# W2 by column halves around batch 1's loads, half output tiles of batch 0, W1 means, folding and denominators in a new order, and batch 1's sums on GpSimd

## The chip, the cores and the metric

The kernel runs on one core of a Trainium2 chip. The metric is device time in microseconds (us), best when low. TensorE does the matmuls ("PE"; its weight loads are "PEld"), VectorE is "DVE", ScalarE "ACT", GpSimd "POOL". The mean clock granted to TensorE is given where it matters. Times of single steps come from the profiled execution, whose span is some 1.8 us shorter than the timed figure.

## The reference, cut to what matters

```python
# B=8 batches, H=8 heads, S=576, D=64, M=32 memory slots; C = H*D = 512, F = 2048
a = softmax(phi, over s)                     # (B,H,S,M)
k_m, v_m = pool(a, k), pool(a, v)            # "pooling": einsum bhsm,bhsd->bhmd
attn = softmax(q @ k_m.T / 8, over m)
x = (attn @ v_m), heads side by side         # (B,S,C): "context products"
xn = (x - mean) / sqrt(var + 1e-6) * g
out = x + relu(xn @ w_ch1) @ w_ch2           # w_ch1: C x F, w_ch2: F x C
```

## The kernel before: the parts that matter here

The kernel doesn't form `xn @ w_ch1` from x. It multiplies each batch's pooled V by W1 once ("folding", `w1b`), adds a term for the mean of W1's columns ("W1 means", `m_sb`), and then multiplies the folded W1 by the normalised attention weights `Eh` (512 products of 288 columns over all batches, `mm1`). `mm2` is the second layer, one output tile of 128 rows at a time, 16 matmuls each. Inputs of a batch are loaded one or two batches ahead. Batches 0 and 1 share tiles: batch 0 is folded while W1 still arrives, and its four output tiles run while batch 1's inputs arrive.

PSUM is handed out as three buffers of two banks ("big") and two of one bank ("one"):

```python
def big(shape, dtype, name):
    return psum.tile(shape, dtype, name=name, tag="big", bufs=3)
def one(shape, dtype, name):
    return psum.tile(shape, dtype, name=name, tag="one", bufs=2)

def w2_load(n):                                  # a quarter of W2's rows, all columns
    nc.gpsimd.dma_start(out=w2b[:, 4*n:4*(n+1), :], in_=w2_v[:, 4*n:4*(n+1), :])
# ... order on the load queue: batch 0, W1 (five pieces), W2, batch 1's phi, K, V, Q

def a_sum(b, ps):                                # sums of the exponents
    if b < 2:
        kv_sum(b, ps)                            # nine matmuls against ones
    else:                                        # GpSimd has added, two matmuls
        ...

# batch 0's W1 stage (cut)
    a_den(0, finish=False); a_tr(0, k_part=False)
    w1_mean(0); m_copy(0); a_w1b(0, 0, 0); a_den2(0)
    ...
    w1_mean(2); m_copy(2); a_w1b(0, 1); mm1(0, 2, 5)
    w1_mean(3); m_copy(3); a_w1b(0, 2); mm1(0, 5, 8)
    ...
# batch 0's output tiles among batch 1's attention (cut)
    mm2(0, 0, 4, 16); mm2(0, 1, 4, 16); mm2(0, 2, 0, 8)
    a_kv(1)                                      # pooling, with the sums first
    mm2(0, 2, 8, 12); a_tr(1); a_qT(1, 0); a_w1b(1, 0)
    mm2(0, 2, 12, 16, finish=False); a_qT(1, 1); a_w1b(1, 1); a_sc(1)
    ...
```

`w1_mean`, `mm2` and the fillers (`warm`, matmuls that only keep TensorE busy) use the one-bank buffers, nearly all else the two-bank ones.

The softmax here doesn't subtract the row's maximum and nothing guards it: scores larger than these inputs give would overflow.

## Time and profile before

| | before |
|---|---|
| time, median | 250.63 us (250.14 to 250.96, three runs; 250.8 over six) |
| span of the profiled execution | 248.8 us |
| TensorE busy | 236.5 us, 95% |
| first context product of batch 0 | 33.08 us |
| first product (`mm1`) of batch 1 | 53.65 us |
| batch 1's product until the next output tile | 8.65 us |

A profile line of the timeline gives start, length, engine, source line, operation, output<-inputs, shapes, count, and in brackets how long the engine stood idle before it and what ended that. The chain of waits follows the last instruction back to what released each step. A row of windows gives length, then busy time of PE, PEld, DVE, ACT and POOL with counts, clock, DMA share and GB/s. The prediction shows most lines that matter of before. Three more are the chain's sum by engine, and from TensorE's timeline the two waits for batch 1's inputs that the change is to remove:

```profile
PE 77%; DMA 17%; issue 2%; ACT 2%; POOL 1%; DVE 0%; POOLq 0%
```

```profile
42.95 0.80 PE L210 MATMUL kv_ps<-kv_bf,e_sb 64*32 64x128 bf16 x72 [0.22 <-DMA kv_bf<-in_v_dram]
...
45.20 0.73 PE L310 MATMUL qT_ps<-ident,q_bf 128*128 128x128 bf16 x10 [0.30 <-DMA q_bf<-in_q_dram]
```

The 17% of DMA is the first 45 us, in which loads keep the queue full.

### The profile page before, as it was taken

What the parts mean: (1) busy time and instruction counts of PE and PEld (TensorE: products, weight loads), DVE (VectorE), ACT (ScalarE), POOL (GpSimd) and SP (SyncE); (2) the same over time, 40 slices, a digit from 0 to 9 for tenths busy, and PEclk for the clock granted to TensorE, in tenths of its full rate; (3) what the DMA queues carried; (4) which work ended last, traced back from release to release, by engine and by line L of the source; (5) the groups of instructions that cost most, each with busy time, mean ns of one, the idle gap of its engine ahead of it and who ended that gap; (6) DMA issues with size and microseconds to landing.
All of it is one profiled execution on the core that took longest, in us unless ns stands there. A gap on an engine that the chain in (4) does not pass through costs nothing.

```text
span 248.8 us, 5860 instructions
## 1 busy us (share of the span) xinstructions
PE 236.5 (95%) x2460; PEld 132.2 (53%) x2491; DVE 156.0 (63%) x304; ACT 130.0 (52%) x219; POOL 60.7 (24%) x100
## 2 busy tenths in 40 slices
PE   7979899999999999999999999999999999999994
PEld 2544554457544665467544674466544764476442
DVE  3247663685577656687569637685679538783641
ACT  3164572587554465837472656655580755465310
POOL 8643241022325402090206202170205001000000
PEclk9999999999999999999999999999999999999999
DMA  7999999998499799919965997429983301203133
GB/s 150 190 202 206 207 256 213 286 223 148 119 174 236 116 216 245 179 20 194 262 122 117 146 242 168 104 37 221 211 167 68 73 14 43 45 12 75 42 84 84
DMA packets 42451, 36.82 MB, mean 148 GB/s; under 512 B 17461, under 2 KB 37689, under 8 KB 42425
## 3 DMA queue, kind: packets, MB, share of 16 engines
q0 software_dynamic: 17776, 19.53, 46.9%
q1 hardware_dynamic: 24488, 16.79, 28.4%
q8 instruction: 19, 0.31, 0.5%
q10 hardware_dynamic: 160, 0.13, 0.2%
q14 instruction: 8, 0.06, 0.1%
HBM read 41.42 MB, written 9.44 MB: 204 GB/s over the span
## 4 chain that ended last, share of the span: by engine, by line
PE 77%; DMA 17%; issue 2%; ACT 2%; POOL 1%; DVE 0%; POOLq 0%
PE ch_ps L481 45%; PE h_ps L411 22%; DMA q_bf<-in_q_dram 8%; DMA w1r<-in_moe_w_ch_dram 6%; DMA kv_bf<-in_k_dram 3%; PE w1b_ps L390 3%; PE o_ps L442 2%; PE last_ps L493 1%; ACT x_sb L448 1%; PE sc_ps L328 1%; PE den_ps L359 1%; PE kv_ps L210 1%; POOL q_bf L92 1%; PE qT_ps L310 0%; ACT qT L313 0%
## 5 line engine op out<-in xcount | busy, mean ns | idle before, releaser
L481 PE MATMUL ch_ps<-w2b,rT 128*128 128x512 bf16 x531 | 123.0, 379 | 2.3 <-issue 1.6
L481 PEld LDWEIGHTS <-rT 128*128 128x128 bf16 x560 | 52.1, 98 | 63.5 <-issue 6.5
L411 PE MATMUL h_ps<-Eh,w1b 128*128 128x288 bf16 x512 | 66.4, 285 | 1.3 <-ACT rT L417 1.0
L417 ACT ACTIVATE rT<-h_ps 128x576 bf16<-128x576 f32 x88 | 52.2, 648 | 26.8 <-PE h_ps L411 26.8
L411 PEld LDWEIGHTS <-w1b 128*128 128x128 bf16 x512 | 49.5, 97 | 18.1 <-issue 2.4
L394 DVE SCALAR_TENSOR_TENSOR w1b<-m_sb,rsum,w1b_ps 128x512 bf16<-128x512 f32 (+1 forms) x66 | 44.2, 726 | 8.5 <-PE w1b_ps L390 6.1
L419 DVE TENSOR_SCALAR rT<-h_ps 128x576 bf16<-128x576 f32 x40 | 30.3, 758 | 25.2 <-PE h_ps L411 24.6
L505 DVE SCALAR_TENSOR_TENSOR x_sb<-ch_ps,rstd,x_sb 128x512 f32<-128x512 f32 x35 | 26.1, 745 | 9.5 <-PE ch_ps L481 6.4
L461 DVE BATCH_NORM_STATS2 bst<-x_sb 128x6 f32<-128x512 f32 x36 | 24.3, 676 | 6.4 <-ACT x_sb L448 6.4
L448 ACT ACTIVATE x_sb<-o_ps 128x1024 f32<-128x1024 f32 (+1 forms) x20 | 17.8, 939 | 16.1 <-PE o_ps L442 16.0
L287 POOL TENSOR_TENSOR vb<-v,vmask 128x256 bf16<-128x256 bf16 x12 | 7.8, 664 | 60.9 <-DVE rs L237 60.9
L194 POOL TENSOR_TENSOR es<-e_sb 128x512 f32<-128x512 bf16 x6 | 6.9, 1156 | 62.2 <-ACT e_sb L187 62.2
L467 ACT ACTIVATE rstd<-mv,eps_sb 128x2 f32<-128x2 f32 (+1 forms) x20 | 5.9, 297 | 30.8 <-DVE mv L462 30.6
L333 ACT ACTIVATE E_sb<-sc_ps,rs 128x640 bf16<-128x640 f32 x16 | 11.8, 790 | 12.8 <-PE sc_ps L328 12.8
L375 DVE SCALAR_TENSOR_TENSOR Eh<-E_sb,rs,rden 128x576 bf16<-128x576 bf16 x16 | 12.4, 814 | 8.8 <-ACT rden L374 8.8
L179 PE MATMUL w_ps<-fill 128*128 128x512 f32 (+1 forms) x16 | 10.5, 774 | 1.6 <-DVE fill L119 1.6
L227 DVE CAST k<-kv_ps 128x256 bf16<-128x256 f32 x7 | 3.0, 425 | 13.8 <-PE kv_ps L210 13.8
L390 PE MATMUL w1b_ps<-w1r,kvT 64*32 64x512 bf16 (+1 forms) x264 | 10.9, 374 | 0.1
L187 ACT ACTIVATE e_sb<-phi_st 128x1152 bf16<-128x1152 f32 x8 | 9.2, 1151 | 2.7 <-DMA phi_st<-in_phi_dram 2.7
L374 ACT ACTIVATE rden<-rden 128x576 f32<-128x576 f32 x16 | 10.0, 672 | 0.1
L92 POOL DMA_DIRECT2D q_bf<-in_q_dram x10 | 7.6, 757 | 4.6 <-DMA w2b<-in_moe_w_ch_dram 1.8
L210 PE MATMUL kv_ps<-kv_bf,e_sb 64*32 64x128 bf16 (+1 forms) x648 | 7.4, 215 | 0.7 <-DMA kv_bf<-in_v_dram 0.4
(76 smaller groups left out, 150.9 us busy)
## 6 DMA issues: line engine op xcount, KB each, us to landing
out_dram<-x_sb SPq DMA_DIRECT2D x70, 128.0 KB, 2.9
kv_bf<-in_k_dram POOLq DMA_DIRECT2D x7, 576.0 KB, 6.1
kv_bf<-in_v_dram POOLq DMA_DIRECT2D x7, 576.0 KB, 9.5
phi_st<-in_phi_dram SPq DMA_DIRECT2D x6, 576.0 KB, 4.9
q_bf<-in_q_dram POOLq DMA_DIRECT2D x6, 576.0 KB, 13.6
w2b<-in_moe_w_ch_dram POOLq DMA_DIRECT2D x4, 512.0 KB, 17.8
w1r<-in_moe_w_ch_dram POOLq DMA_DIRECT2D x3, 512.0 KB, 14.2
q_bf<-in_q_dram POOLq DMA_DIRECT2D x4, 288.0 KB, 12.6
```

The costliest lines, as they stand in the source:

```text
L179: nc.tensor.matmul(w_ps[:, 0:N], fill[:, 0:P], fill[:, 0:N], start=True, stop=True)
L333: nc.scalar.activation(out=E_[:, g].rearrange("p (a x) -> p a x", a=2), in_=sc[:, :, 0:HP], func=AF.Exp, scale=s["rs"][:, g:g + 1])
L375: nc.vector.scalar_tensor_tensor(out=Eh[:, g, :], in0=s["E"][:, g, 0:S], scalar=s["rs"][:, g:g + 1], in1=rd[:, g].rearrange("p a x -> p (a ...
L390: nc.tensor.matmul(ps[32 * j:32 * (j + 1), g, 0:N], s["kvT"][r:r + 64, 2, 32 * j:32 * (j + 1)], w1r[r:r + 64, j, fs], start=True, stop=Tru ...
L394: nc.vector.scalar_tensor_tensor(out=s["w1b"][:, g, fs], in0=m_sb[:, fs], scalar=s["rsum"][:, g:g + 1], in1=ps[:, g, 0:N], op0=ALU.mult, o ...
L411: nc.tensor.matmul(h_ps[:, half, 0:HS], s["w1b"][:, g, P * j:P * (j + 1)], s["Eh"][:, g, HS * half:HS * (half + 1)], start=(g == 0), stop= ...
L417: nc.scalar.activation(out=dst, in_=h_ps[:, :, 0:HS], func=AF.Relu)
L419: nc.vector.tensor_scalar(out=dst, in0=h_ps[:, :, 0:HS], scalar1=0.0, scalar2=None, op0=ALU.max)
L448: nc.scalar.activation(out=x[:, 0:n].rearrange("p i (u y) -> p i u y", u=2), in_=o_ps.rearrange("p u (i y) -> p i u y", i=2)[:, 0:n], func ...
L461: nc.vector.bn_stats(out=stt, in_=x)
L481: nc.tensor.matmul(ch_ps, rT[:, j, P * t:P * (t + 1)], w2b[:, j, :], start=(j == 0), stop=(j == JC - 1))
L505: nc.vector.scalar_tensor_tensor(out=x, in0=ch_ps, scalar=rstd, in1=x, op0=ALU.mult, op1=ALU.add)
```

## The change

The intent: batch 1's V and Q should not have to queue behind all of W2, of which batch 0's first output tiles need one half only. So W2 is loaded by column halves, the second half behind batch 1's Q, and batch 0's four tiles are computed as eight half tiles, all first halves ahead of batch 1's attention. At the same time batch 0's W1 stage is reordered (means and folding a piece ahead of the products, folding into the one-bank buffers), the denominators go head half by head half, and batch 1's sums of exponents move to GpSimd.

```diff
-    def w2_load(n):
-        nc.gpsimd.dma_start(out=w2b[:, 4 * n:4 * (n + 1), :], in_=w2_v[:, 4 * n:4 * (n + 1), :])
+    def w2_load(h, n):
+        nc.gpsimd.dma_start(out=w2b[:, 4 * n:4 * (n + 1), C2[h]],
+                            in_=w2_v[:, 4 * n:4 * (n + 1), C2[h]])
...
     for n in range(4):
-        w2_load(n)
+        w2_load(0, n)
     phi1 = load_phi(1, nc.gpsimd)
     kv1 = load_kv(1)
     q1 = load_q(1)
     loaded[1] = (phi1, kv1, q1)
+    for n in range(4):
+        w2_load(1, n)
...
-        if b >= 2:                    # GpSimd adds the exponents
+        if b >= 1:
...
-        if b < 2:
+        if b < 1:
             kv_sum(b, ps)
...
+        if ones:                      # folding into both one-bank buffers
+            ps = [one([P, 512], FP32, "w1b_ps") for _ in range(2)]
...
+    def mm2h(t, h, j0, j1):           # half an output tile
+        if j0 == 0 and (h == 1 or t % 2 == 0):
+            halfs[h] = one([P, 2, C // 2], FP32, "ch_ps")
...
-    w1_mean(2); m_copy(2); a_w1b(0, 1); mm1(0, 2, 5)
-    w1_mean(3); m_copy(3); a_w1b(0, 2); mm1(0, 5, 8)
+    mm1(0, 2, 4, (0,)); w1_mean(2); m_copy(2); mm1(0, 2, 4, (1,)); a_w1b(0, 1, ones=True)
+    w1_mean(3); m_copy(3); mm1(0, 4, 6); a_w1b(0, 2, ones=True)
...
+    mm2h(2, 0, 0, 16); mm2h(3, 0, 0, 16); mm2h_out(2, 0); mm2h_out(3, 0)
+    a_kv(1); a_qT(1, 0); a_tr(1); a_qT(1, 1)
+    mm2h(0, 1, 0, 4); a_sc(1); a_w1b(1, 0); load(2)
...
+    a_eh(1, 1); a_w1b(1, 2)
+    mm2h(0, 1, 12, 16); mm2h_out(0, 1)
+    mm2h(1, 1, 12, 16); mm2h_out(1, 1)
+    mm2h(2, 1, 0, 16); a_exp(2); a_w1b(1, 3)
+    mm2h(3, 1, 0, 16); mm2h_out(2, 1); a_vb(1); mm2h_out(3, 1)
```

(Statements that stand on lines of their own are joined here, comments are added, and lines are cut.)

More of the change, by code (lines that the diff above doesn't have):

```diff
@@ L102 @@
     w2_v = moe_w_ch2.rearrange("(j p) c -> p j c", p=P)
-    def w2_load(n):
-        nc.gpsimd.dma_start(out=w2b[:, 4 * n:4 * (n + 1), :], in_=w2_v[:, 4 * n:4 * (n + 1), :])
+    C2 = (slice(0, C // 2), slice(C // 2, C))
+    def w2_load(h, n):
+        nc.gpsimd.dma_start(out=w2b[:, 4 * n:4 * (n + 1), C2[h]],
+                            in_=w2_v[:, 4 * n:4 * (n + 1), C2[h]])
     phi0 = load_phi(0)
@@ L261, in a_tr @@
         s = st8[b]
-        t_ps = big([P, 3, P], BF16, "kvT_ps")
+        t_ps = (big if k_part else one)([P, 3, P], BF16, "kvT_ps")
         if k_part:
@@ L335, in a_sc, with den_tiles @@
         s["E"] = E_
-    def a_den(b, finish=True):
+    def den_tiles(b):
         s = st8[b]
-        Eh = att.tile([P, 2, S], BF16, name="Eh", bufs=3)
-        rd = att.tile([P, 2, 2, HS], FP32, name="rden", bufs=1)
-        if b < 2:
-            for g in range(2):
-                den = big([P, 2, 512], FP32, "den_ps")
-                for half in range(2):
-                    o = HS * half
-                    nc.tensor.matmul(den[:, half, 0:HS], blk, s["E"][:, g, o:o + HS],
-                                     start=True, stop=True)
-                nc.scalar.activation(out=rd[:, g], in_=den[:, :, 0:HS], func=AF.Ln)
-        else:
-            den = [big([P, 2, 512], FP32, "den_ps") for _ in range(2)]
-            E_ = s["E"]
-            for half in range(2):
-                cs = slice(HS * half, HS * (half + 1))
-                for r in (0, D):
-                    for g in range(2):
-                        o = r if g == 0 else D - r
-                        nc.tensor.matmul(den[g][o:o + D, half, 0:HS], blk[r:r + D, r:r + D],
-                                         E_[r:r + D, g, cs], start=True, stop=True,
-                                         tile_position=(r, o))
-            nc.scalar.activation(out=rd[:, 0], in_=den[0][:, :, 0:HS], func=AF.Ln)
-            for r in (0, D):
-                nc.scalar.activation(out=rd[r:r + D, 1], in_=den[1][D - r:P - r, :, 0:HS],
-                                     func=AF.Ln)
-        s["Eh"], s["rd"] = Eh, rd
-        if finish:
-            a_den2(b)
@@ new lines, in den_tiles, with a_den_g @@
+        s["Eh"] = att.tile([P, 2, S], BF16, name="Eh", bufs=3)
+        s["rd"] = att.tile([P, 2, 2, HS], FP32, name="rden", bufs=1)
+        return s["rd"]
+    def a_den_g(b, g):
+        s = st8[b]
+        rd = den_tiles(b) if g == 0 else s["rd"]
+        den = big([P, 2, 512], FP32, "den_ps")
+        for half in range(2):
+            o = HS * half
+            nc.tensor.matmul(den[:, half, 0:HS], blk, s["E"][:, g, o:o + HS],
+                             start=True, stop=True)
+        nc.scalar.activation(out=rd[:, g], in_=den[:, :, 0:HS], func=AF.Ln)
+        nc.scalar.activation(out=rd[:, g], in_=rd[:, g], func=AF.Exp, scale=-1.0)
@@ new lines, in a_den @@
+    def a_den(b):
+        rd = den_tiles(b)
+        den = [big([P, 2, 512], FP32, "den_ps") for _ in range(2)]
+        E_ = st8[b]["E"]
+        for half in range(2):
+            cs = slice(HS * half, HS * (half + 1))
+            for r in (0, D):
+                for g in range(2):
+                    o = r if g == 0 else D - r
+                    nc.tensor.matmul(den[g][o:o + D, half, 0:HS], blk[r:r + D, r:r + D],
+                                     E_[r:r + D, g, cs], start=True, stop=True,
+                                     tile_position=(r, o))
+        nc.scalar.activation(out=rd[:, 0], in_=den[0][:, :, 0:HS], func=AF.Ln)
+        for r in (0, D):
+            nc.scalar.activation(out=rd[r:r + D, 1], in_=den[1][D - r:P - r, :, 0:HS],
+                                 func=AF.Ln)
@@ L370, in a_den2, with a_eh @@
+    def a_eh(b, g):
+        s = st8[b]
+        nc.vector.scalar_tensor_tensor(
+            out=s["Eh"][:, g, :], in0=s["E"][:, g, 0:S],
+            scalar=s["rs"][:, g:g + 1], in1=s["rd"][:, g].rearrange("p a x -> p (a x)"),
+            op0=ALU.mult, op1=ALU.mult)
     def a_den2(b):
-        s = st8[b]
-        Eh, rd = s["Eh"], s["rd"]
+        rd = st8[b]["rd"]
         for g in range(2):
             nc.scalar.activation(out=rd[:, g], in_=rd[:, g], func=AF.Exp, scale=-1.0)
-            nc.vector.scalar_tensor_tensor(
-                out=Eh[:, g, :], in0=s["E"][:, g, 0:S],
-                scalar=s["rs"][:, g:g + 1], in1=rd[:, g].rearrange("p a x -> p (a x)"),
-                op0=ALU.mult, op1=ALU.mult)
@@ L380, in a_w1b @@
-    def a_w1b(b, n, part=None):
+            a_eh(b, g)
+    def a_w1b(b, n, part=None, ones=False, evict=True):
         s = st8[b]
@@ L383, in a_w1b @@
             s["w1b"] = att.tile([P, 2, F], BF16, name="w1b", bufs=1)
-        ps = big([P, 2, 512], FP32, "w1b_ps")
+        if ones:
+            ps = [one([P, 512], FP32, "w1b_ps") for _ in range(2)]
+        else:
+            ps2 = big([P, 2, 512], FP32, "w1b_ps")
+            ps = [ps2[:, g] for g in range(2)]
         fs = slice(512 * n, 512 * (n + 1)) if part is None else W1C[part]
@@ L390, in a_w1b, with out, mm1_g, mm1 @@
                 nc.tensor.matmul(
-                    ps[32 * j:32 * (j + 1), g, 0:N], s["kvT"][r:r + 64, 2, 32 * j:32 * (j + 1)],
+                    ps[g][32 * j:32 * (j + 1), 0:N], s["kvT"][r:r + 64, 2, 32 * j:32 * (j + 1)],
                     w1r[r:r + 64, j, fs], start=True, stop=True, tile_position=(r, 32 * j))
-        for g in range(2):
+        def out(g):
             nc.vector.scalar_tensor_tensor(
                 out=s["w1b"][:, g, fs], in0=m_sb[:, fs], scalar=s["rsum"][:, g:g + 1],
-                in1=ps[:, g, 0:N], op0=ALU.mult, op1=ALU.add)
+                in1=ps[g][:, 0:N], op0=ALU.mult, op1=ALU.add)
+        if not evict:
+            return out
+        for g in range(2):
+            out(g)
     pair = {}
-    def mm1(b, j0, j1):
+    hs = {}
+    def mm1_g(b, j, g):
         s = st8[b]
-        if b % 2 == 0 and j0 == 0:
+        if g == 0:
+            hs[j] = big([P, 2, 512], FP32, "h_ps")
+        for half in range(2):
+            nc.tensor.matmul(
+                hs[j][:, half, 0:HS], s["w1b"][:, g, P * j:P * (j + 1)],
+                s["Eh"][:, g, HS * half:HS * (half + 1)],
+                start=(g == 0), stop=(g == 1))
+    def mm1(b, j0, j1, gs=(0, 1)):
+        if b % 2 == 0 and j0 == 0 and 0 in gs:
             pair[b // 2] = moe.tile([P, JC, 2 * S], BF16, name="rT", bufs=1)
@@ L407, in mm1 @@
         for j in range(j0, j1):
-            h_ps = big([P, 2, 512], FP32, "h_ps")
-            for g in range(2):
-                for half in range(2):
-                    nc.tensor.matmul(
-                        h_ps[:, half, 0:HS], s["w1b"][:, g, P * j:P * (j + 1)],
-                        s["Eh"][:, g, HS * half:HS * (half + 1)],
-                        start=(g == 0), stop=(g == 1))
+            for g in gs:
+                mm1_g(b, j, g)
+            if 1 not in gs:
+                continue
+            h_ps = hs[j]
             dst = rT[:, j, off:off + S].rearrange("p (a x) -> p a x", a=2)
@@ L484, in mm2, with mm2h_out @@
             mm2_out(pr, t)
+    halfs = {}
+    def mm2h(t, h, j0, j1):
+        if j0 == 0 and (h == 1 or t % 2 == 0):
+            halfs[h] = one([P, 2, C // 2], FP32, "ch_ps")
+        if j0 == 0:
+            chs[(t, h)] = halfs[h][:, 0 if h else t % 2, :]
+        for j in range(j0, j1):
+            nc.tensor.matmul(chs[(t, h)], pair[0][:, j, P * t:P * (t + 1)],
+                             w2b[:, j, C2[h]], start=(j == 0), stop=(j == JC - 1))
+    def mm2h_out(t, h):
+        x, rstd = xs[(0, t)]
+        nc.vector.scalar_tensor_tensor(out=x[:, C2[h]], in0=chs[(t, h)],
+                                       scalar=rstd, in1=x[:, C2[h]], op0=ALU.mult, op1=ALU.add)
+        if h == 1:
+            x_out(0, t, x)
     def mm2_last(pr, t):
@@ L506, in mm2_out, with x_out @@
                                        op0=ALU.mult, op1=ALU.add)
+        x_out(pr, t, x)
+    def x_out(pr, t, x):
         for u in range(2):
@@ L534 @@
     v_out(0, v_ps[:, :, 0:D])
-    a_den(0, finish=False)
+    a_den_g(0, 0)
     a_tr(0, k_part=False)
+    a_den_g(0, 1)
     w1_mean(0)
     m_copy(0)
-    a_w1b(0, 0, 0)
-    a_den2(0)
-    warm(1, 256)
+    fold = a_w1b(0, 0, 0, evict=False)
+    fold(0)
+    a_eh(0, 0)
+    fold(1)
+    a_eh(0, 1)
+    warm(1)
     w1_mean(1)
     m_copy(1)
-    a_w1b(0, 0, 1)
-    warm(1, 256)
-    mm1(0, 0, 2)
+    mm1(0, 0, 2, (0,))
+    a_w1b(0, 0, 1, ones=True)
+    mm1(0, 0, 2, (1,))
+    mm1(0, 2, 4, (0,))
     w1_mean(2)
     m_copy(2)
-    a_w1b(0, 1)
-    mm1(0, 2, 5)
+    mm1(0, 2, 4, (1,))
+    a_w1b(0, 1, ones=True)
     w1_mean(3)
     m_copy(3)
-    a_w1b(0, 2)
-    mm1(0, 5, 8)
+    mm1(0, 4, 6)
+    a_w1b(0, 2, ones=True)
+    mm1(0, 6, 8)
     w1_mean(4)
     m_copy(4)
-    a_w1b(0, 3)
-    mm1(0, 8, 11)
+    mm1(0, 8, 9)
+    a_w1b(0, 3, ones=True)
     a_vb(0)
-    mm1(0, 11, 16)
+    mm1(0, 9, 16)
     x_tiles(0, [0, 1])
     x_tiles(0, [2, 3])
-    mm2(0, 0, 0, 4)
-    mm2(0, 1, 0, 4)
+    mm2h(0, 0, 0, 16)
     x_rstd(0, [0, 1])
+    a_exp(1)
+    mm2h(1, 0, 0, 16)
+    mm2h_out(0, 0)
+    mm2h_out(1, 0)
     x_rstd(0, [2, 3])
-    a_exp(1)
-    mm2(0, 0, 4, 16)
-    mm2(0, 1, 4, 16)
-    mm2(0, 2, 0, 8)
+    mm2h(2, 0, 0, 16)
+    mm2h(3, 0, 0, 16)
+    mm2h_out(2, 0)
+    mm2h_out(3, 0)
     a_kv(1)
-    mm2(0, 2, 8, 12)
+    a_qT(1, 0)
     a_tr(1)
-    a_qT(1, 0)
+    a_qT(1, 1)
+    mm2h(0, 1, 0, 4)
+    a_sc(1)
     a_w1b(1, 0)
-    mm2(0, 2, 12, 16, finish=False)
-    a_qT(1, 1)
+    load(2)
+    mm2h(1, 1, 0, 4)
+    mm2h(0, 1, 4, 8)
+    a_den_g(1, 0)
     a_w1b(1, 1)
-    a_sc(1)
-    mm2_out(0, 2)
-    mm2(0, 3, 0, 4)
-    a_w1b(1, 2)
-    a_den(1)
-    load(2)
+    mm2h(1, 1, 4, 8)
+    a_den_g(1, 1)
+    a_eh(1, 0)
+    mm2h(0, 1, 8, 12)
+    mm2h(1, 1, 8, 12)
+    a_eh(1, 1)
+    a_w1b(1, 2)
+    mm2h(0, 1, 12, 16)
+    mm2h_out(0, 1)
+    mm2h(1, 1, 12, 16)
+    mm2h_out(1, 1)
+    mm2h(2, 1, 0, 16)
     a_exp(2)
-    mm2(0, 3, 4, 12)
     a_w1b(1, 3)
-    mm2(0, 3, 12, 16, finish=False)
+    mm2h(3, 1, 0, 16)
+    mm2h_out(2, 1)
     a_vb(1)
-    mm2_out(0, 3)
+    mm2h_out(3, 1)
     a_qT(2, 0)
@@ L651 @@
         if more:
-            a_den(nb, finish=False)
+            a_den(nb)
         mm2_out(pr, t[1])
```

## The prediction

> **What bounds the kernel now.** I read the page first, then the chain of waits, then windows and timelines of the stretch that the change touches.
>
> ```profile
> PE 236.5 (95%) x2460; PEld 132.2 (53%) x2491; DVE 156.0 (63%) x304; ACT 130.0 (52%) x219; POOL 60.7 (24%) x100
> ```
>
> TensorE (PE) is busy nearly throughout, so only its idle time, or time given to useless work, can be won. The chain says where that lies:
>
> ```profile
> 10.52 15.11 DMA w1r<-in_moe_w_ch_dram
> 25.62 0.29 issue
> 25.91 19.24 DMA q_bf<-in_q_dram
> 45.15 0.05 issue
> 45.20 0.73 PE qT_ps L310 x10
> ...
> 53.81 0.57 PE h_ps L411 x4
> 54.39 0.02 issue
> 54.41 0.66 ACT rT L417
> 55.07 0.04 issue
> 55.11 7.13 PE h_ps L411 x56
> ```
>
> Columns: start, length, what held the chain. Up to 45 us it runs through the load queue (W1, W2, then batch 1's phi, K, V, Q, in order); after that it is PE. From the first product of batch 1 (h_ps, 53.65) on, PE is full, and the diff leaves that part alone. So the change is decided by when PE reaches this product, and by how well it then runs. Two windows split the start at the first context product of batch 0 (33.1):
>
> ```profile
> 16.40:33.10 16.70, 15.34 (x131) 8.88 (x132) 12.38 (x22) 9.96 (x18) 5.22 (x8) 1.00 1.25 206
> 33.10:53.65 20.55, 19.71 (x234) 9.77 (x237) 12.17 (x25) 11.55 (x19) 2.55 (x4) 1.00 1.18 248
> ```
>
> (PE, PEld, DVE, ACT, POOL busy, clock, DMA share, GB/s.) The clock is full. PE's busy time counts pipeline latency, so I count issue time. First window: W1 means 3.5 us (8 matmuls of 0.115, 12 of 0.216), folding 1.5, fillers 0.9, 64 products of 0.124 are 8.0: 13.9 of 16.7. Second: 64 output matmuls of 0.216 are 13.8, all else some 5.6: 19.4 of 20.55. So 2.8 and 1.1 us are the most that better order could give, 1.6% together.
>
> **What the Trainium skill says.** "TensorE: Matmul & The Clock Gate", Back-to-back issue gap: a warm matmul of N columns takes N/2.4 + 2.5 ns alone, and streams with weight loads have other figures (131 ns at N=512). The trace agrees with the first: 8 output matmuls take 1.73 us in the chain (216 ns at 512), 64 products 7.96 us (124 ns at 288). So I take 0.1105 us at 256: halving a tile costs only 0.005 us a pair. "PSUM — Partial Sum Buffer", Engine vs sequencer instructions: the queues of VectorE, ScalarE and GpSimd are strict FIFO. The timelines show these engines in program order; my prediction rests on it. The same page, Specifications (TRN2): 8 banks of 2 KiB. The code has 3 buffers of two banks and 2 of one: all 8 are taken, so whoever takes a one-bank buffer takes it from another. "DMA: Bandwidth & Descriptors", Specifications: at least 512 B for line rate. W2 halves write rows of 512 B, just there. The trace's packets of the first two W1 pieces, of that size, take 59 ns, those of 1024 B 95 ns: 196 against 206 GB/s in 2 us stretches. Halving W2 costs some 0.5 us of queue.
>
> **The change part by part.**
>
> *Loads.* W2's second halves go behind batch 1's Q. W1 is in at 25.6; four halves of about 1.3 us, phi 1.55 (as now), K 2.65, V and Q some 6: V lands near 38 (now 42.9), the Qs near 39 and 41 (now 45.15 and 47.1), W2 complete near 46. The DMA wait in the chain goes. That is the intent, and I believe it.
>
> *Batch 0's W1 stage.* The same matmuls, but now folding takes both one-bank buffers, which the W1 means use too. I followed the three engines by hand, folding 0.70 us (0.44 at 256 columns), evictions 0.65 on ACT and 0.76 on DVE, copy of means 0.60. Denominators by halves bring Eh's first half to 18.7 (now 19.2), its second stays at 19.95. Then: 0.45 waiting for that half; 0.35 for the first eviction (the fourth open h tile needs a fourth big buffer); 0.35 for the copy of means that frees the second fold buffer; 0.95 for the fold that frees the bank of the third means (PE done 23.4, fold until 24.3); 0.3 for the copy of the last means; 0.35 before piece 13; with 0.35 before the first Eh, 3.1 idle against 2.8 now. The last W1 piece lands at 25.6 and is not used before 27. The stage ends at 33.4, now 33.1: no gain.
>
> *Batch 0's first halves.* Context products 0.65, 64 matmuls of 0.1105 are 7.1: PE is at batch 1's pooling 7.7 us after the stage's end, at 41.1. But batch 1's sums of exponents now come from GpSimd instead of nine matmuls (saves 0.3), and the pooling waits for them first. Their way now, from ACT and POOL timelines:
>
> ```profile
> 36.58 0.29 ACT L467 ACTIVATE rstd<-mv,eps_sb 128x2 f32<-128x2 f32 x1 [0.86 <-DVE mv L462]
> ```
>
> ```profile
> 54.04 1.16 POOL L194 TENSOR_TENSOR es<-e_sb 128x512 f32<-128x512 bf16 x1 [15.65 <-ACT e_sb L187]
> 55.28 0.94 POOL L196 TENSOR_TENSOR es<-es 128x256 f32<-128x256 f32 x1
> 56.30 0.45 POOL L197 TENSOR_TENSOR es<-es 128x128 f32<-128x128 f32 x1
> 56.83 0.43 POOL L198 TENSOR_TENSOR es<-es,e_sb 128x128 f32<-128x128 f32 x1
> 57.32 0.29 POOL L200 CAST hl<-es 128x128 bf16<-128x128 f32 x1
> 57.70 0.43 POOL L201 TENSOR_TENSOR hl<-es,hl 128x128 bf16<-128x128 f32 x1
> ```
>
> The rstd starts 3.5 us after the stage's end (behind copies and statistics). The exponential follows it: 0.5 + 1.15. The six GpSimd steps (here batch 2's) run from 54.04 to 58.13, 4.1 us. Sum with hand-overs 9.4 us: PE waits 9.4 - 7.7 = 1.7 us. Pooling starts at 42.8 (now 42.2 for the sums, 42.95 for K and V): what the loads gave is taken by this.
>
> *Second halves.* From pooling (t = 0): pooling 0.8, key copy on ACT until 1.3, first Q transposes until 1.45, their copy of 1.24 until 2.8, the next 0.7 until 3.5. The scores need both, and PE has only transposes and four half matmuls before: 0.7 us idle. First folding at 3.85. Then PE goes through two folding pieces, two denominators, 24 half matmuls, a third folding and 8 more, until 8.5. DVE has two pairs of folds (1.4 each), Eh's halves (0.8 each, the second behind ACT's four passes, 8.0), then the third pair:
>
> ```profile
> 46.34 1.40 DVE L394 SCALAR_TENSOR_TENSOR w1b<-m_sb,rsum,w1b_ps 128x512 bf16<-128x512 f32 x2 [0.73 <-PE w1b_ps L390]
> ...
> 52.37 1.55 DVE L375 SCALAR_TENSOR_TENSOR Eh<-E_sb,rs,rden 128x576 bf16<-128x576 bf16 x2 [0.70 <-ACT rden L374]
> ```
>
> 4.35 to 7.25 for two pairs, Eh until 8.85, third pair until 10.25, and only then the output of tile 0's second half, about 0.43, until 10.7. Tile 2's second half needs its bank: the second halves are four one-bank tiles in two buffers. PE stands from 8.5 to 10.75, 2.25 us. Then 1.8 + 0.35 + 1.8: batch 1's product starts at 14.6.
>
> *Sum.* 33.4 + 9.4 + 14.6 = 57.4, now 53.65: 3.75 later. In return batch 1's product no longer stops after two tiles (8.65 us until the next outputs at 62.3, against 7.96 in batch 2), as exponentials, folds and Eh are done before it: 0.65 back. Cross-check: idle 1.7 + 0.7 + 2.25 against 1.1 now is +3.5, halves +0.25, sums -0.3, stage +0.3, the product -0.65: 3.1 us slower. 250.63 + 3.1 = 253.7; as the intent speaks the other way and my count of 17 us by hand can err by a microsecond, I say 253.3.
>
> **Rivals.** (1) The intent holds: the DMA wait goes and nothing takes its place. For it: the chain's 19 us on Q. Against it: PE had only some 0.3 us idle for Q, because W2 work filled the wait. It would need all waits removed: 248 to 250. (2) Only one of the two new waits is real, say because GpSimd finishes sooner or DVE gets to the output earlier: 251 to 252. Both follow from program order and measured durations, so this is less likely. (3) The W1 stage gets faster: idle down to half, 1.5 us less, hence 252. (4) It gets slower, with DVE late for evictions, or 256-column matmuls take 0.13 for their weight loads: 2.5 us for 128, 255.5 to 256. PE's 64-odd ns transposes with as many weights speak against that.
>
> **Range and chances.** The two waits give 4 us, the W1 stage is open to +-1. From one wait gone and a better stage to both in full with a worse stage: 250.8 to 255.4. 2% is 5.0 us. Faster by that needs more than all idle time there is (3.9): 0.02. Slower needs 1.5 us beyond my sum: 0.09. Within: 0.89.
>
> **What would show it.** PE's gap before batch 1's pooling with GpSimd's last sum as releaser (1.7); its gap before the third second-half tile with DVE as releaser (2.2); V and Q of batch 1 landing before PE is ready; 16 half matmuls in 1.77 us; the stage of batch 0 ending at 33.4; batch 1's product starting near 57.4 and taking 8.0; later stages shifted, alike. I am wrong if pooling starts at once after the first halves, if a DVE backlog doesn't hold tile 2, or if the first product starts before 53.

## The result, and the profile after

The changed kernel takes 254.0 us (median of six runs, 253.78 to 257.24); before took 250.8 us in the same rounds. The ratio is 1.0157, 95% interval 1.0116 to 1.0197. Ratios here are the mean time of one kernel's runs over that of the other's of the same rounds, so not quite the ratio of the medians. Four of the six runs lie between 253.78 and 254.08; the others, 255.64 and 257.24, had a mean clock of 0.99 and 0.987.

Page of the changed kernel, busy times and the chain by engine:

```profile
PE 237.0 (94%) x2519; PEld 138.3 (55%) x2546; DVE 156.8 (62%) x308; ACT 130.3 (52%) x219; POOL 66.9 (27%) x110
...
PE 81%; ACT 6%; DVE 4%; DMA 4%; POOL 3%; issue 2%; POOLq 0%; DVEq 0%
```

TensorE does 0.5 us more in a span 3.3 us longer. DMA has fallen from 17% of the chain to 4%: the loads are no longer what the chain runs through. In its place stand ACT, DVE and POOL. The chain of the changed kernel shows where (start, length, what):

```profile
37.82 1.06 ACT e_sb L192
...
38.96 1.16 POOL es L199
...
42.39 0.44 POOL hl L206
...
43.05 0.73 PE kv_ps L215 x72
...
50.94 0.82 DVE Eh L378
51.76 1.32 DVE w1b L408 x2
53.08 0.41 DVE x_sb L527
...
53.53 1.91 PE ch_ps L522 x16
...
57.63 7.96 PE h_ps L427 x64
```

First: exponential, GpSimd's additions, and only then batch 1's pooling. Second: `Eh`, a pair of folds and the output of tile 0's second half on DVE, and only then TensorE's tile 2. After 57.63 it is TensorE alone, as before. The timeline of TensorE in the changed kernel puts numbers to these waits and shows a third, in the W1 stage:

```profile
24.53 1.02 PE L170 MATMUL m_ps<-w1r,gneg 128*128 128x512 bf16 x4 [0.93 <-DVE w1b L408]
...
33.79 0.71 PE L470 MATMUL o_ps<-vb,Eh 64*128 64x128 bf16 x16
34.44 7.16 PE L522 MATMUL ch_ps<-w2b,rT 128*128 128x256 bf16 x64
42.36 0.18 PE L256 MATMUL kv_ps<-ones,hl 128*128 128x2 bf16 x1 [0.76 <-POOL hl L205]
42.87 0.18 PE L256 MATMUL kv_ps<-ones,hl 128*128 128x2 bf16 x1 [0.33 <-POOL hl L206]
...
53.53 1.91 PE L522 MATMUL ch_ps<-w2b,rT 128*128 128x256 bf16 x16 [1.88 <-DVE x_sb L527]
```

The bracket counts from the end of the last result in the pipeline; from the last matmul's issue the gaps are a little longer. The 64 first-half matmuls follow each other at 0.109 us and end their issue near 41.5, and pooling starts at 42.98: 1.5 us, less one tiny matmul between. The gap before tile 2 is some 2.0 us.

Adding up by the profiles' landmarks, changed minus before: the scores of batch 0, which nothing changed, start 0.17 later (14.36 against 14.19, loads differ that much from run to run); from there to the first context product 19.43 against 18.89, +0.54; from that to batch 1's first product (57.46 against 53.65) 23.67 against 20.57, +3.10; that product until the next output tile 8.18 against 8.65, -0.47 (both profiles lack the record of that tile's first matmul, 7 of 8 are there; in e1_kvsum, where it is there, the distance is 7.95, so the true ones are some 0.2 shorter and the difference stands); the remainder 186.46 against 186.50. The sum is +3.3, the difference of the spans (252.1 and 248.8).

### The profile page after: what moved, and what is told of

Its sections match the earlier page's. It is cut to its first block, busy times and chain, and to the rows that moved or that the text cites. A ratio compares the mean times of both kernels' runs of the same rounds, so it can differ in the third digit from the quotient of the medians.

```text
span 252.1 us, 5995 instructions
## 1 busy us (share of the span) xinstructions
PE 237.0 (94%) x2519; PEld 138.3 (55%) x2546; DVE 156.8 (62%) x308; ACT 130.3 (52%) x219; POOL 66.9 (27%) x110
## 4 chain that ended last, share of the span: by engine, by line
PE 81%; ACT 6%; DVE 4%; DMA 4%; POOL 3%; issue 2%; POOLq 0%; DVEq 0%
PE ch_ps L509 42%; PE h_ps L427 25%; DMA kv_bf<-in_v_dram 4%; PE w1b_ps L403 3%; PE ch_ps L522 2%; PE o_ps L470 2%; ACT x_sb L476 2%; PE last_ps L539 1%; PE kv_ps L215 1%; PE sc_ps L333 1%; PE m_ps L170 1%; ACT rT L445 1%; DVE w1b L408 1%; PE den_ps L368 1%; DVE Eh L378 1%
## 5 line engine op out<-in xcount | busy, mean ns | idle before, releaser
L509 PE MATMUL ch_ps<-w2b,rT 128*128 128x512 bf16 x470 | 108.5, 379 | 2.0 <-issue 1.4
L509 PEld LDWEIGHTS <-rT 128*128 128x128 bf16 x496 | 46.2, 98 | 56.4 <-issue 5.8
L551 DVE SCALAR_TENSOR_TENSOR x_sb<-ch_ps,rstd,x_sb 128x512 f32<-128x512 f32 x31 | 23.1, 745 | 7.5 <-PE ch_ps L509 4.5
L199 POOL TENSOR_TENSOR es<-e_sb 128x512 f32<-128x512 bf16 x7 | 8.1, 1155 | 57.8 <-ACT e_sb L192 57.8
L522 PE MATMUL ch_ps<-w2b,rT 128*128 128x256 bf16 x128 | 15.3, 273 | 1.9 <-DVE x_sb L527 1.9
L522 PEld LDWEIGHTS <-rT 128*128 128x128 bf16 x128 | 12.1, 98 | 4.5 <-issue 3.1
L232 DVE CAST k<-kv_ps 128x256 bf16<-128x256 f32 x7 | 3.0, 425 | 13.8 <-PE kv_ps L215 13.8
L403 PE MATMUL w1b_ps<-w1r,kvT 64*32 64x512 bf16 (+1 forms) x264 | 11.5, 374 | 0.0
L184 PE MATMUL w_ps<-fill 128*128 128x512 f32 x14 | 9.9, 828 | 1.6 <-DVE fill L122 1.6
```

Of the source, the lines that this page charges most:

```text
L403: nc.tensor.matmul(ps[g][32 * j:32 * (j + 1), 0:N], s["kvT"][r:r + 64, 2, 32 * j:32 * (j + 1)], w1r[r:r + 64, j, fs], start=True, stop=Tru ...
L509: nc.tensor.matmul(ch_ps, rT[:, j, P * t:P * (t + 1)], w2b[:, j, :], start=(j == 0), stop=(j == JC - 1))
L522: nc.tensor.matmul(chs[(t, h)], pair[0][:, j, P * t:P * (t + 1)], w2b[:, j, C2[h]], start=(j == 0), stop=(j == JC - 1))
L551: nc.vector.scalar_tensor_tensor(out=x, in0=ch_ps, scalar=rstd, in1=x, op0=ALU.mult, op1=ALU.add)
```

## The experiments

Theory: the time comes from two new waits, one for GpSimd's sums (A), one for a bank behind DVE's work (B), and a little from the W1 stage (C); the new order of loads itself works. Rivals: the waits are only symptoms and would come back elsewhere; the halving of tiles costs; or the order of loads is worth nothing. All experiments gave correct results. In the table, "stretch" is the time from batch 0's first context product to batch 1's first product in the profile (20.57 before, 23.67 changed), and "full clock" are the times of runs with a mean clock of 0.997 or more.

| run | what | stretch | median | ratio to before (95%) | full clock |
|---|---|---|---|---|---|
| changed | | 23.67 | 254.0 | 1.0157 (1.0116 to 1.0197) | 253.78 to 254.08, 4 of 6 |
| e1_kvsum | A undone: sums on TensorE | 22.43 | 252.78 | 1.0097 (1.0058 to 1.0136) | 252.38 to 252.84, 3 of 4 |
| e2_sumlate | A moved: sums taken late | 24.24, clock halved | 254.62 | 1.0133 (1.0078 to 1.0188) | 252.52, 1 of 4 |
| e3_bigtile | B away: other buffer | 21.62 | 251.74 | 1.0044 (1.0017 to 1.0072) | 251.47 to 251.88, 4 of 4 |
| e6_outfirst | B eased: order on DVE | 22.35 | 252.57 | 1.0080 (1.0051 to 1.0109) | 252.31 to 252.96, 4 of 4 |
| e4_w1before | C undone | 23.68 | 254.22 | 1.0133 (1.0068 to 1.0198) | 253.08 and 253.61, 2 of 4 |
| e5_w1big | C: folds in big buffers | 23.67 | 254.29 | 1.0119 (1.0051 to 1.0188) | 253.13 and 253.74, 2 of 4 |
| e7_loads | order of loads undone | 25.79, clock halved | 255.93 | 1.0213 (1.0154 to 1.0272) | none of 4 |
| e8_both | A moved and B away | 20.60 | 250.81 | 0.9993 (0.9940 to 1.0046) | 250.12 to 251.21, 4 of 4 |
| e9_best | e8, C undone, two details | 20.82 | 250.52 | 0.9997 (0.9975 to 1.0020) | 250.12 to 250.84, 6 of 6 |
| e10_bestold | e9 with loads as before | 25.95, clock halved | 254.31 | 1.0161 (1.0125 to 1.0197) | 254.47, 1 of 6 |
| e11_fill | changed, B filled | 23.66 | 254.17 | 1.0145 (1.0116 to 1.0175) | 253.76 to 254.27, 4 of 5 |
| e12_bestpe | e9 with A undone | 20.65 | 250.95 | 1.0011 (0.9986 to 1.0036) | 250.30 to 251.24, 4 of 6 |

### A: the wait for GpSimd's sums

e1_kvsum gives batch 1's sums back to TensorE.

```diff
-        if b >= 1:
+        if b >= 2:
...
-        if b < 1:
+        if b < 2:
             kv_sum(b, ps)
```

> The changed kernel with one part undone: batch 1's sums of exponents again by nine matmuls on TensorE. Theory (TensorE waits 1.5 us for GpSimd's last sum before pooling): pooling starts near 41.6 in place of 42.98, the nine matmuls take 0.3 of it, everything behind follows, batch 1's product starts near 56.5 (57.6), span near 251.0 (252.1), time 1.1 us under the changed kernel's. Rival (pooling would start no sooner, because the exponential or the load of V comes no sooner): pooling stays near 42.9, and the time rises by 0.3 us or stays.

Timeline of TensorE in this run:

```profile
41.54 0.37 PE L223 MATMUL kv_ps<-ones,e_sb 128*128 128x2 bf16 x9
41.84 0.80 PE L215 MATMUL kv_ps<-kv_bf,e_sb 64*32 64x128 bf16 x72
```

No wait stands before the nine matmuls, they take 0.3 us, and pooling follows. The stretch is 1.24 us shorter, the span 250.9. The theory said 1.1, which this bears out, and the rival (pooling could not start sooner) is out.

e2_sumlate leaves the sums to GpSimd, but takes them behind pooling and transposes.

```diff
-    a_kv(1)
-    a_qT(1, 0); a_tr(1)
-    a_qT(1, 1)
+    kv_ps1 = big([P, 2, 512], FP32, "kv_ps")
+    kv_mm(1, kv_ps1, slice(0, 2)); k_out(1, kv_ps1, True); v_out(1, kv_ps1[:, :, D:2 * D])
+    a_qT(1, 0); a_tr(1)
+    a_sum(1, kv_ps1); rs_out(1, kv_ps1)
+    a_qT(1, 1)
```

> The changed kernel, sums still on GpSimd, but the two matmuls that take them come after pooling, the first Q transposes and the K and V transposes. Theory: the wait of 1.5 us is only one of order, pooling starts near 41.5, no wait on GpSimd is left over 0.2 us, product of batch 1 starts near 56.2, span near 250.6, 0.3 us better than with the sums on TensorE. Rival (what follows is held by something else that came no sooner, as the copies of Q on ACT): pooling starts earlier but the product of batch 1 starts at 57.0 or later, span over 251.5.

The wait for GpSimd is gone, but another took part of its place, and the expectation missed it. The pooled K and V now stay in their two-bank buffer until the late sums are out, so the second Q transposes wait for another one, that of the K and V transposes (TensorE's timeline; in e9_best below, where the sums have a bank of their own, this wait is gone):

```profile
44.99 0.72 PE L315 MATMUL qT_ps<-ident,q_bf 128*128 128x128 bf16 x10 [0.64 <-DVE kvT L279]
```

From the first context product to tile 2's second half it takes 18.72 us against 19.74 in the changed kernel: 1.0 us won of the 1.5 expected. The span is useless as a comparison (253.6), because the clock fell to half twice in this execution. Once was right after gap B; the windows before and after 53.80:

```profile
50.39:53.80 3.41, 1.52 (x20) 1.11 (x13) 3.31 (x6) 1.50 (x2) 1.75 (x2) 1.00 1.22 208
53.80:57.21 3.41, 3.41 (x24) 1.83 (x21) 0.00 (x0) 0.00 (x0) 1.72 (x5) 0.50 1.16 268
```

The clock is the third figure from the right. In the second window tile 2's 16 half matmuls took 3.27 us; they took 1.91 in the changed kernel's profile. The one run of this kernel at full clock, 252.52, is 1.3 us under the changed kernel's full-clock runs, the same as e1_kvsum within the spread. So A is a matter of order, as thought, but the way it was undone here wins no more than undoing it on TensorE.

### B: the wait for a bank behind DVE's queue

e3_bigtile gives tile 2's second half a two-bank buffer.

```diff
-            halfs[h] = one([P, 2, C // 2], FP32, "ch_ps")
+            halfs[h] = (big if h and t == 2 else one)([P, 2, C // 2], FP32, "ch_ps")
```

> The changed kernel, only that tile 2's second half takes a two-bank buffer and so doesn't wait for tile 0's output on DVE. Theory (the 1.9 us gap before it is the wait for that bank, behind DVE's folds): the gap goes, product of batch 1 starts near 55.7, span near 250.2, 1.9 us under the changed kernel. Rival (DVE's backlog is what counts, it only shows at another place: the third fold, the fourth fold's buffer or tile 3): the gap moves behind tile 2, under 0.7 us are won, span over 251.4.

TensorE's timeline now runs through the second halves of tiles 0, 1 and 2 without a break:

```profile
50.42 2.79 PE L522 MATMUL ch_ps<-w2b,rT 128*128 128x256 bf16 x24
53.15 0.41 PE L403 MATMUL w1b_ps<-w1r,kvT 64*32 64x512 bf16 x8
```

The stretch is 2.05 us shorter, and the time 251.74. DVE's work is the same as in the changed kernel, so its backlog as such was not the bound: TensorE only stood because it needed the bank that DVE came to last.

e6_outfirst keeps the buffers, and moves the third pair of folds behind the outputs, so that DVE gets to that bank sooner. (The eight folding matmuls move on TensorE too.)

```diff
     a_eh(1, 1)
-    a_w1b(1, 2)
     mm2h(0, 1, 12, 16); mm2h_out(0, 1)
     mm2h(1, 1, 12, 16); mm2h_out(1, 1)
+    a_w1b(1, 2)
```

> The changed kernel, same buffers, but the third folding piece of batch 1 comes after the outputs of tiles 0 and 1 in the program, so that DVE writes tile 0's half first. Theory: DVE gets to that output near 51.8 instead of 53.0, the gap before tile 2 shrinks from 1.9 to some 0.7 us, span near 250.9. Rival (the gap belongs to the exponents and Eh ahead of the third fold, not to the fold): the gap shrinks by less than 0.5 us, span over 251.6.

```profile
52.63 1.91 PE L522 MATMUL ch_ps<-w2b,rT 128*128 128x256 bf16 x16 [0.67 <-DVE x_sb L527]
```

The gap is 0.67 where 0.7 was expected, and the stretch is 1.32 us shorter. The two parts of the gap come apart here: the third pair of folds ahead of the output makes 1.3 us of it, and 0.7 is left, with `Eh` still ahead of the output on DVE.

### A and B together

e8_both has the edits of e2_sumlate and e3_bigtile.

> Both waits taken away at once: sums taken late, and tile 2's second half in a two-bank buffer. Theory (the two waits add up, 1.5 + 1.9): product of batch 1 near 54.3, span near 248.8, that is, the kernel before within 0.3%, perhaps a little under it. Rival (one hides the other, what is won by the first is lost at the second): span over 249.8.

The stretch is 20.60, as good as before's 20.57, and the ratio 0.9993. So A and B are not hidden by each other (2.05 + 1.02 = 3.07 won, and 23.67 - 20.60 = 3.07). The span was 0.4 over the expectation; its first context product came 0.2 later than in the changed kernel's profile, since batch 0's loads did, and the 0.64 wait of e2_sumlate is in it too.

### C: the W1 stage

e4_w1before puts batch 0's denominators, means, folding, fillers and products back into the order of before.

```diff
-    fold = a_w1b(0, 0, 0, evict=False)
-    fold(0); a_eh(0, 0); fold(1); a_eh(0, 1)
-    warm(1); w1_mean(1); m_copy(1)
-    mm1(0, 0, 2, (0,)); a_w1b(0, 0, 1, ones=True); mm1(0, 0, 2, (1,)); ...
+    a_w1b(0, 0, 0); a_den2(0); warm(1, 256)
+    w1_mean(1); m_copy(1); a_w1b(0, 0, 1); warm(1, 256); mm1(0, 0, 2)
+    w1_mean(2); m_copy(2); a_w1b(0, 1); mm1(0, 2, 5)
+    ...
```

> The changed kernel with batch 0's W1 stage (means, folding, fillers, denominators) as in the kernel before. Theory (the new order wins nothing, its waits are as long): the stage ends near 33.2 in place of 33.8, span near 251.5, 0.5 us under the changed kernel. Rival (the new order does win, and the earlier loads would have hurt the old one): the stage ends at 34 or later, span 252.1 or more.

From batch 0's scores to its first context product this run takes 18.89 us, exactly as before, where the changed kernel takes 19.43; the span is 251.3. The new order of this stage costs 0.54 us. The figures are steady: in the profiles with the new stage and no change of the clock in it (changed, e1, e3, e6, e7, e8, e11) the stage took 19.43 or 19.44, in those with the old one (before, e4, e9, e10, e12) 18.88 or 18.89.

e5_w1big keeps the new order, with folds in one two-bank buffer each.

```diff
-    a_w1b(0, 0, 1, ones=True)
+    a_w1b(0, 0, 1, ones=False)
     (the same for the three later pieces)
```

> The changed kernel, only that batch 0's folding pieces take one two-bank buffer each, as before, instead of both one-bank buffers. Theory (the 0.93 us wait of the third means is for a one-bank buffer that a fold holds): that wait goes, and so do those for the copies of means (0.3 each), but the products' tiles now lack a third buffer and wait 0.3 us several times; the stage ends between 32.9 and 33.6, span 251.2 to 251.9. Rival (DVE's folds and ACT's copies bound the stage, whoever holds the buffers): the stage ends at 33.8 or later, span 252.1 or more.

The wait of 0.93 us before the means `w1_mean(3)` is gone: in TensorE's timeline they come straight behind the fold.

```profile
24.67 0.41 PE L403 MATMUL w1b_ps<-w1r,kvT 64*32 64x512 bf16 x8
25.01 1.04 PE L170 MATMUL m_ps<-w1r,gneg 128*128 128x512 bf16 x4
```

That wait was for the bank. The stage as a whole can't be read from this profile (it ended at 35.06), as the clock was at half from 16.84 to 20.25. But the part from the first means of 512 columns on ran at full clock, and took 11.84 us (23.22 to 35.06) against 12.31 in the changed kernel (21.48 to 33.79). In e2_sumlate, whose clock had fallen at nearly the same place, it took 12.31 too, with the wait (0.92) in it; so the clock is not what removed it. So in this part the bank costs some 0.5 us, net of the shorter waits that came in (0.24 and twice 0.25). What the earlier part does at full clock is not shown. The two runs at full clock, 253.13 and 253.74 against the changed kernel's mean of 253.9, agree, but are too few to show it.

### The order of loads

e7_loads loads W2's second halves right behind the first.

```diff
     for n in range(4):
         w2_load(0, n)
+    for n in range(4):
+        w2_load(1, n)
     phi1 = load_phi(1, nc.gpsimd)
```

(The later loop is taken out.)

> The changed kernel, but W2's second halves are loaded right behind its first, ahead of batch 1's inputs, as before. Theory (the new order of loads does what it is meant to, and would win on its own): V lands near 43.4 and the Q halves near 45.2 and 46.5 in place of 38.1, 39.8 and 41.1, the first Q transposes wait until 45.2 (now 43.7), product of batch 1 near 59.2, span near 253.6, 1.5 us over the changed kernel. Rival (the order of loads is worth nothing, since the waits behind it cover it): span within 0.4 of 252.1.

```profile
43.85 0.80 PE L215 MATMUL kv_ps<-kv_bf,e_sb 64*32 64x128 bf16 x72 [0.61 <-DMA kv_bf<-in_v_dram]
44.91 1.05 PE L315 MATMUL qT_ps<-ident,q_bf 128*128 128x128 bf16 x10 [0.26 <-DMA q_bf<-in_q_dram]
```

V now holds pooling (43.85 for 42.98), and Q its transposes (44.91 for 43.71): 0.9 and 1.2 us lost to the loads. The rest of the 2.1 us of span I put down to the clock, which was at half from 45.16 to 48.58 here. All four timed runs had 0.992 or less, and the changed kernel's own run at 0.99 took 255.64 against 255.75 to 257.42 here, so the times alone don't tell the loads from the clock. By the profile the new order of loads is worth 1.2 us where the transposes start, even with A and B in the way; that the rival is out rests on this and on e10_bestold below.

### Towards a better kernel, and what it leaves

e9_best joins what helped: e8_both, the W1 stage of before, a bank of its own for the late sums, and four half matmuls ahead of the scores.

```diff
+    a_qT(1, 1)
+    sum_ps = one([P, 1, 256], FP32, "sum_ps")
+    a_sum(1, sum_ps); rs_out(1, sum_ps)
+    mm2h(0, 1, 0, 4); mm2h(1, 1, 0, 4)
     a_sc(1)
```

> What the runs so far point to: the changed kernel's loads and half tiles, with batch 0's W1 stage of before (0.75 us better in the run with it alone), GpSimd's sums taken after all transposes into a one-bank buffer of their own (no wait for them, and none for the buffer that the run with late sums still held, 0.64), tile 2's second half in a two-bank buffer (2.0), and four half matmuls moved ahead of the scores (0.35). Theory, by adding the parts: stage ends near 33.1, product of batch 1 starts near 52.9 (57.46 in the changed kernel, 53.65 before), span near 247.5, time near 249.3, 0.5% under the kernel before. Rival (the waits come back elsewhere, as at the scores behind ACT's copies of Q): span over 248.8, no better than before.

```profile
44.39 1.03 PE L522 MATMUL ch_ps<-w2b,rT 128*128 128x256 bf16 x8 [0.58 <-DVE qT L319]
45.35 0.47 PE L333 MATMUL sc_ps<-qT,kvT 64*32 64x320 bf16 x16
```

The rival was right that the waits come back elsewhere, but not at the scores. The one-bank buffer that the sums took is missing for tile 0's second half, which now waits 0.58 us for DVE's copy of Q. The scores follow straight behind these eight half matmuls (45.35); ACT's copies of Q are done by 44.71. So they start 11.72 us after the first context product, against 11.34 in e8_both with four half matmuls ahead, and the stretch stays at 20.82. The time ties with before (0.9997). Adding single gains, I had expected 0.5% under it. Batch 1's product came 1.5 us later than expected (54.45 for 52.9): 1.0 of it is this stretch, and most of the rest is a later start, batch 0's scores at 14.75 (14.36 in the changed kernel; 14.06 to 14.79 in all profiles).

e12_bestpe has the sums on TensorE instead (the edit of e1_kvsum) and the rest of e9_best.

> As the first of these, but batch 1's sums by nine matmuls on TensorE, as before the change. Theory (GpSimd's sums are worth 0.3 us of TensorE if nothing waits for them, no more): product of batch 1 near 53.2, span near 247.8, 0.2 to 0.3 us over the first. Rival (with the exponents early, TensorE's sums cost nothing since the scores wait for ACT's copies anyway): equal to the first, or better.

The stretch is 20.65, so TensorE's nine matmuls cost nothing beside e9_best, as its rival said. The rival's reason isn't what the trace shows: ACT's copies are done by 44.61, before the scores at 44.89. What makes up for the nine matmuls is e9_best's wait of 0.58, of which some 0.3 is left here. The ratio is 1.0011: no gain either, though its product of batch 1 runs 0.5 us better than before's. No version here beats the kernel before by more than the times can tell (95%: 0.9975 to 1.0020 for e9_best, 0.9986 to 1.0036 here).

e10_bestold is e9_best with the loads of e7_loads.

> The same, but W2's second halves loaded ahead of batch 1's inputs, as before. Theory (without the other waits the order of loads counts in full): TensorE is at pooling near 40.8 and waits for V until 43.4 and for Q until 45.2, product of batch 1 near 55.6, span 2.5 us or more over the run before, and the clock falls in some runs in the long wait. Rival (order of loads is worth at most the 1.5 us of the earlier run): span under 249.2.

```profile
43.65 1.16 PE L215 MATMUL kv_ps<-kv_bf,e_sb 64*32 64x128 bf16 x72 [2.78 <-DMA kv_bf<-in_v_dram]
```

With the other waits gone TensorE stands 2.78 us for V, the clock then falls to half for 6.83 us, and the time is 254.31, 3.8 us over e9_best. This is what the order of loads is worth with half tiles, the fallen clock included; the one run at full clock took 254.47. It is worth nothing against the kernel before, which has no half tiles, loads in the old order and still ties with e9_best: its tile work at that place covers all but 0.5 us of the wait.

### The clock

e11_fill puts four useless fp32 matmuls into gap B of the changed kernel.

```diff
     mm2h_out(1, 1)
+    fl = big([P, 2, 512], FP32, "fl_ps")
+    for _ in range(4):
+        nc.tensor.matmul(fl[:, 0, 0:256], fill[:, 0:P], fill[:, 0:256], start=True, stop=True)
     mm2h(2, 1, 0, 16)
```

> The changed kernel with four filler matmuls (fp32, 256 columns, 0.45 us each by the fillers of batch 0, result unused) in the gap before tile 2's second half. They don't shorten the way to the end. Theory (the gap of 1.9 us is long enough for the clock to be halved for 3.4 us in some executions, and this makes the runs of 255 and 257 us): all six runs between 253.6 and 254.4 with a clock of 0.995 or more. Rival (the clock falls at the start, or of itself): some runs at 255 or more as before.

The wait before tile 2 is down to 0.15, the stretch is the same (23.66), and four of the five runs lie within 253.76 to 254.27 at a clock of 0.999 or more. The fifth had 0.99 and took 254.81, so the expectation of a full clock in all runs was missed, by one run that was only 0.6 us slower. No run was at 255 or above, where the changed kernel had two of six. This fits the theory that gap B lets the clock fall in some executions (seen directly in e2_sumlate), but five runs against six don't prove that it made the two slow ones; those were not profiled. All runs together say more: with gap B at its full length (changed, e1, e2, e4, e5) 10 of 22 had a mean clock of 0.993 or less, with it gone, shortened or filled (e3, e6, e8, e9, e11, e12) 3 of 29. So the gap makes a fall likelier, but it isn't the only place: in e2_sumlate the clock also fell at 16.25 us and in e5_w1big at 16.84, in the W1 stage, as the rival has it. Before itself had a mean clock of 0.986 to 0.993 in 6 of 25 runs, and in four of them its time was as usual.

## Why the prediction was right

It said 253.3 us within 250.8 to 255.4, from a sum of 253.7; the median was 254.0.

*The W1 stage.* "The stage ends at 33.4": it ended at 33.79, of which 0.17 is a later start. It costs 0.54 us where the working had 0.3. The wait of 0.95 for the bank of the third means came as 0.93, and e5_w1big shows that it is for the bank. "No gain" was right.

*First halves and the wait for the sums.* Predicted 7.7 us to be ready for pooling, 9.4 until GpSimd was done. Measured: 7.7 and 9.2 (33.79 to 41.5 and to 42.98). The wait was 1.5, predicted 1.7. e1_kvsum shows it: 1.24 us back, with the nine matmuls in it.

*Second halves.* Predicted 14.6 us from pooling to batch 1's product; measured 14.5 (42.98 to 57.46). The gap before tile 2 was 2.0 against 2.25, and both its cause (the bank) and its make-up (folds and `Eh` ahead of the output on DVE) hold by e3_bigtile and e6_outfirst. The idle time before the scores was 0.35 by the timeline rather than 0.7, so this term was too large. The rule it all rested on, strict FIFO on ACT, DVE and POOL ("PSUM — Partial Sum Buffer", Engine vs sequencer instructions), agrees with the timelines read here, which show these engines in program order: e6_outfirst changes that order and wins 1.3 us.

*Half matmuls.* 0.1105 us was assumed. The gap rule of "TensorE: Matmul & The Clock Gate", Back-to-back issue gap, gives 0.1092 for 256 columns, and the trace has 0.109 from start to start. So halving tiles is nearly free: 128 x 0.109 = 14.0 us against 64 x 0.216 = 13.8.

*Loads.* V, the Qs and the end of W2 landed at 38.05, 39.8, 41.1 and 46.4 by the trace, predicted 38, 39, 41 and 46. W2 in halves cost 0.56 us more of the queue than in quarters (10.75 against 10.19), predicted 0.5. (The packet times that the prediction reads as 59 and 95 ns are 60 and 98 in the trace.)

*What was given back.* Batch 1's product ran in 7.96 us without its stop after two tiles, as predicted; counted from its first matmul it won 0.47 us, predicted 0.65. The working took 8.65 for before, which ends at the second matmul of the next tile as the first one's record is missing, and so counted 0.2 too much. Later stages only shifted (186.46 against 186.50).

The errors of the terms are small and partly cancel, which is luck: the stage cost 0.24 more than its term and the product gave back 0.18 less, while the way to pooling was 0.2 and the one from there 0.1 shorter; the change in span was 3.3 us, the sum said 3.1. The shading of the figure down to 253.3, for the sake of the intent, was not needed. What the working did not have at all is the clock: it said that the clock is full, and in some executions of the changed kernel it was not.

## What to carry to other kernels

Bringing a load forward only pays if TensorE has nothing else to do while it waits: here the kernel before filled the wait with output tiles, so the gain was bounded by the 0.5 us for which TensorE stood (0.22 for V, 0.30 for Q), while every engine that the new order put between two TensorE steps (GpSimd's sums, DVE's output behind folds) became a wait of its own. Before moving work to an idle engine, or adding tiles to a pool of two buffers, follow that engine's queue in program order up to the instruction that frees the buffer: here this gave both waits to within 0.3 us. Gains of gaps closed one at a time don't always add up, either: as e9_best shows, a buffer taken for one wait is missing at the next.

## What the Trainium skill lacked or had wrong

- "TensorE: Matmul & The Clock Gate", HAM oscillation: the rule given is "no PE-idle gaps >~3.4µs". It is not enough here. In e2_sumlate the clock fell to half after a stretch of 3.41 us in which TensorE was busy for 1.52, with no gap over some 2.1 us. The page also tells of short idles between matmuls that make the clock swing, but gives no share of busy time at which it falls. The runs give none either: in the changed kernel's profile a stretch of the same length, across the same gap (51.24 to 54.65), with 1.53 busy was not followed by a fall. What decides between the two stays open. The length of the throttled time, 3.41 us or twice that (in e10_bestold), agrees with the page's window, and so do the places: in all 14 profiles every change of the clock comes a whole number of 3.41 us after its first rise.
- The same page, Back-to-back issue gap: 131 ns per matmul at N=512 is given for streams of weight load and matmul. Such streams took 215 to 216 ns here in both kernels, and 109 ns at N=256; the page's isolated formula, N/2.4 + 2.5, is the one that holds.
- "DMA: Bandwidth & Descriptors", Specifications: 512 B is given as the size for line rate. It held closely. The page works its cost per packet out for 256 B only (Why small descriptors are slow), and gives no measured figure for 512 B on this chip: W2's first halves, in rows of 512 B, landed every 1.34 to 1.37 us, and whole quarters of W2, in rows of 1024 B, every 2.5 to 2.6 us in the kernel before, so some 5 to 6% more per byte.
